# Making x + h once, along the tokens, and turning it by DMA, in a fused attention and mixer kernel

## The chip, the cores and the metric

One core of a Trainium2 chip. The engines named here are TensorE (PE, with its weight loads PEld), VectorE (DVE), ScalarE (ACT), GpSimd (POOL) and SyncE (SP), which issues the DMAs. The metric is device time in microseconds (us) of one execution; lower is better.

## The reference

Two operators in a row, for 8 batches of S = 3136 tokens, width 256, in fp32:

```
scores = (z @ z.T) / S                      # z: S x 64
x      = u * (relu(scores)**2 @ v)          # gated attention, S x 256
h      = (x.T @ U @ V).T                    # low rank 32 across the tokens
x2     = x + h
out    = x2 + relu(x2 @ w_ch1) @ w_ch2      # 256 -> 1024 -> 256
```

h needs the sum over all tokens of a batch (x.T @ U), so the second operator of a batch can start only when the batch's attention is done.

## The kernel before

**Tiling.** 3136 tokens are 24 tiles of 128 and a tail of 64. Tokens are worked on in groups of four tiles (512 tokens), so a batch has six full groups, 0 to 5, and one small group, 6, of 64 tokens. A batch and a group make an item: 56 items, and the loop over t runs nine steps longer.

**What one step t does.** The attention of item t (`av_stream`: 96 units of 256 columns, one unit being a pair of concurrent matmuls on the two halves of the array's rows; `av_end` adds the last token tile, and `av_out`, L575, multiplies by u into `x_bf`), the scores of later items (`score_burst`), the first layer `ch1_part` and the second layer `ch2_stream` (32 units) of the item eight steps back, and x + h of the item seven steps back. A small group's attention is `av_small`, its second layer `ch2_small`. Scores are squared (L301) and, where needed a second time, turned by block DMA transposes on SP (L327). In the last nine steps only the two layers run; in the first seven only attention.

**The two ways.** Each half of the rows writes one PSUM bank at a time. In way 0 half 0 writes bank 0 and half 1 bank 1, in way 1 crosswise. A stream runs all its units in one way, then the others. Between, the function `post` (L153) puts a no-op on POOL that waits for the last matmuls, and the next matmul of that accumulator waits for the no-op.

**x + h, made two ways.** `t1_all` makes t1 = x.T U once per batch. Then, for each group, h is made twice. `u2T_unit` makes it turned (features on the rows, tokens along the columns: one pair of 512 columns) and adds xT in L665; xT is `x_bf` turned by a DMA, L608, issued by `x_turn` at the start of the step before. The result `u2T` is what the first layer reads. `ch2_begin` makes h again along the tokens (two pairs of 256 columns), as the start of the second layer's accumulator. When that is full, L765 adds `x_bf` into `out_sb` (fp32) and L767 stores it.

**The order.** Nothing reorders instructions: the program emits them in the order in which a planner in Python calls them, and each engine runs its own queue in order. The planner counts PE units as time (`clock`), books estimated busy time of ACT, DVE and SP (`book`), gives out four PSUM tiles (`take_ps`) and puts off work until it is due (`hold`, `run_held`). `emit` walks the light units of a step (attention, then second layer) and puts the queues' entries (first layer, scores, x + h) at their places; an entry that needs free PSUM tiles is put off by up to 14 units until `ps_ready`. `cast` goes to ACT or DVE, whichever is booked less.

The end of a step's stream, before:

```
        qm.append((nA, -1, False, finish))             # av_end, then ch2_begin
        ...
        qm.append((nA + nC // 2, -1, False, between))  # scores, then u2T_unit
        emit((av.units if av else []) + ch2, [qc, qs, qm], av, av_box)
```

Of the kernel before, what the change touches and what calls it, by code (L numbers as in the profile page):

```python
# [18 lines left out]
def kernel(  # L19
# [52 lines left out]
    V4_bf = persist.tile([P, S], BF16, name="V4_bf")  # L72
# [3 lines left out]
    lasts, smalls, xs, t1s, u2Ts, relus = {}, {}, {}, {}, {}, {}  # L76
# [103 lines left out]
    def cast(out, in_, n):  # L180

        if free_at["act"] <= free_at["dve"]:
            book("act", clock[0], n / 110)
            nc.scalar.copy(out=out, in_=in_)  # L184
        else:
            book("dve", clock[0], n / 130)
            nc.vector.tensor_copy(out=out, in_=in_)  # L187
# [271 lines left out]
    class Ways:  # L459
        def __init__(self, total, way, step):  # L460
            self.total, self.way, self.step = total, way, step
            self.at = [0, 0]
            self.units = [self.unit] * (2 * total)
# [23 lines left out]
    def av_stream(b, g, box):  # L487
        def lhs(h, q, jt):
            jb, j = divmod(jt, GT)
            while (b, jb) not in v_cast:  # L490
                run_held(min(h[0] for h in held))
            while (b, g, jb) not in blocks:
                if (g, jb, b) in ready_turns:
                    issue_turn((g, jb, b))
                else:
                    run_held(min(h[0] for h in held))
            t = blocks[b, g, jb][1]
            if jb >= g or made_twice(b, g):
                while squared.get((b, g, jb), 0) < 2:
                    run_held(min(h[0] for h in held))  # L500
                return t[h, j, q * P : (q + 1) * P]

            return t.rearrange("p a c -> p (a c)")[h, (q * GT + j) * P : (q * GT + j + 1) * P]

        per = 2 * GT

        def step(i, way, first, least):
            if first:
                xs[b, g] = pool.tile([P, GT, D], BF16, name="x_bf", bufs=10)
                box["k"], box["ps"] = take_ps()  # L510
            jt, a = divmod(i, 2)
            pair(
                box["k"],
                crossed(
                    way,
                    a,
                    lambda h, q: dict(
                        out=four(box["ps"])[:, q, :],
                        lhsT=lhs(h, q, jt),
                        rhs=v_bfs[b][h, jt, :],  # L520
                        start=first,
                        stop=False,
                    ),
                ),
                D,
            )
            while box.get("given", 0) < least // per:
                give_block(blocks[b, g, box.get("given", 0)])
                box["given"] = box.get("given", 0) + 1

        return Ways(2 * NF, 1, step)

    def av_small(b, g):
        k, ps = take_ps()
        rows = groups[g][1]
        xs[b, g] = pool.tile([P, GT, D], BF16, name="x_bf", bufs=10)
# [65 lines left out]
    def x_turn(b, g):  # L604
        n = len(tiles_of(g))
        rows = min(P, groups[g][1])
        xT = pool.tile([P, GT, ND, P], BF16, name="xT", bufs=2)
        nc.sync.dma_start_transpose(  # L608
            out=xT[:, :n, :, :rows].rearrange("p q d c -> p (q d) c"),
            in_=xs[b, g][:rows, :n, :].rearrange("p q d -> p (q d)"),  # L610
        )
        xTs[b, g] = xT
# [25 lines left out]


    def u2T_unit(b, g):  # L640
        g0, gw = groups[g]
        n = len(tiles_of(g))
        rows = min(P, gw)
# [20 lines left out]
        u2T = pool.tile([P, ND, GT, P], BF16, name="u2T", bufs=3)  # L664
        nc.vector.tensor_tensor(  # L665
            out=u2T[:, :, :n, :rows],
            in0=ps[:, :, :gw].rearrange("p d (q c) -> p d q c", c=rows),
            in1=xTs[b, g][:, :n, :, :rows].rearrange("p q d c -> p d q c"),
            op=ALU.add,
        )  # L670
        u2Ts[b, g] = u2T

    def ch1_part(b, g, h0, way, box):

        g0, gw = groups[g]
        if way == 0:
            if h0 == 0:
                relus[b, g] = [take_block() for _ in range(NH // GT)]
            box[h0] = take_ps()
        k, ps = box[h0]  # L680
        for db in range(ND):
            ops = []
            for h in range(2):
# [7 lines left out]
                            out=ps[:, bank, :gw],  # L691
                            lhsT=w1_bf[h * hp : (h + 1) * hp, db, ht * P : (ht + 1) * P],
                            rhs=u2Ts[b, g][h * hp : (h + 1) * hp, db].rearrange("p q c -> p (q c)")[:, :gw],
# [18 lines left out]
    def ch2_begin(b, g, box):  # L712

        box["k"], box["ps"] = take_ps()
        t0 = groups[g][0] // P
        for a in range(2):
            pair(
                box["k"],
                crossed(
                    0,  # L720
                    a,
                    lambda h, q: dict(
                        out=four(box["ps"])[:, q, :],
                        lhsT=V4_bf[h, (t0 + q) * P : (t0 + q + 1) * P],
                        rhs=t1s[b][h, :],
                        start=(a == 0),
                        stop=False,
                    ),
                ),
                D,  # L730
            )

    def ch2_stream(b, g, box):
        def step(i, way, first, least):
            k, a = divmod(i, 2)
# [9 lines left out]
                        start=False,  # L745
# [7 lines left out]
            if least == 2 * NH:  # L753
                ps_free[box["k"]] = book("dve", clock[0] + 3, 11.2)
                ch2_out(b, g, four(box["ps"]), P, pool.tile([P, GT, D], FP32, name="out_sb"))

        return Ways(2 * NH, 0, step)

    def ch2_out(b, g, acc, rows, o):
# [4 lines left out]
        n, t0 = len(ts), ts[0][1]  # L764
        nc.vector.tensor_tensor(out=o, in0=acc, in1=xs[b, g][:rows, :n, :], op=ALU.add)  # L765
# [4 lines left out]
    def ch2_small(b, g):  # L770
        k, ps = take_ps()
        g0, rows = groups[g]
        nc.tensor.matmul(
            out=ps[:rows, 0, :D],
            lhsT=V4_bf[:hp, g0 : g0 + rows],
            rhs=t1s[b][:hp, :],
            start=True,
            stop=False,
            tile_position=(0, 0),
        )  # L780
        for kt in range(NH):
            c = kt % 2
            for h in range(2):
# [4 lines left out]
                    start=(kt < 2 and (h, c) != (0, 0)),  # L788
# [3 lines left out]
        pe(NH / 2 + 3)  # L792
        o = pool.tile([P, GT, D], FP32, name="out_sb")
        four_sums(k, ps, o[:rows, 1:3, :])
        ch2_out(b, g, o[:rows, 1:2, :], rows, o[:rows, 0:1, :])
        book("dve", clock[0] + 3, 3)

    def emit(light, queues, av=None, av_box=None, slack=14):
# [5 lines left out]
        def issue(queue):  # L804
            place, need, turn, unit = queue.pop(0)
            if turn and av and any(av.at):
                post(av_box["k"])
                av.turn()
            unit()
            run_held()  # L810

        queues = [sorted(q, key=lambda h: h[0]) for q in queues]
        for i, f in enumerate(light):
# [9 lines left out]
            if av and av.stuck():  # L823
# [3 lines left out]
                else:  # L827
                    post(av_box["k"])
# [49 lines left out]
    def load_V(i0):  # L878
        todo = []
        n = P // 4  # L880
        for i in range(i0, i0 + 2):
# [5 lines left out]
            def casts(i=i, entry=entry, raw=raw):  # L887
# [5 lines left out]
                if i == 3:  # L893
                    cast(V4_bf[:, NF * P :], raw[:, n * NF : n * NF + S - NF * P], 100)
# [9 lines left out]
        4: lambda: load_w(0),  # L904
        5: lambda: load_w(1) + load_U(),
# [77 lines left out]
    for t in range(n_items):  # L983
        jobs = todo[t]
        n_end = 0 if t == 0 else min(len(jobs), 2 if t % NG == NQ else 1)
        if t >= NG and t % NG == 0:
            n_end = 0
# [4 lines left out]
    for t in range(n_items + NG + 2):  # L992
# [14 lines left out]
        if 0 <= t - NG + 1 < n_items:  # L1007
            x_turn(*items[t - NG + 1])
        for i, f in enumerate(casts_next):
            hold(clock[0] + 15 + 15 * i, f)  # L1010
# [29 lines left out]
        turns_at = (16, 48, nA - 8)  # L1040
        if av and full:

            for h, x, y in zip(hs, (4, 22, 36, 62), (16, 32, 48, nA - 8)):
# [4 lines left out]
        elif av:  # L1048
# [9 lines left out]
            qs += [(x, k, True, lambda: scores(k)) for x in turns_at if k]  # L1058
        else:

            order = []
            for h in range(0, NH if mix else 0, 4):
                if att and h:
                    order.append(lambda: av_small(*att))
                order += [one(h, 0), one(h + 2, 0)] + mine[:1] + [one(h, 1), one(h + 2, 1)]
                mine = mine[1:]
            if att and not mix:
                order.append(lambda: av_small(*att))
            order += mine
            if att:  # L1070
                qc += [(0, 0, False, f) for f in order]
            else:
                n = max(nC, 1)
                qc += [(n * i / len(order) + (t == n_items) * 4, 1, False, f) for i, f in enumerate(order)]
        if u2i and u2i[1] == 0:
            qm.append((0.4 * nA, 1, False, lambda: t1_all(u2i[0])))
            if av:
                qm.append((0.7 * nA, 1, False, lambda: u2T_unit(*u2i)))

        def finish():  # L1080
            if av:
                av_end(*att, av_box)
            if nC:
                ch2_begin(*fin, ch2_box)

        def between():

            if end:
                score_burst(end)
            if u2i and att and not (av and u2i[1] == 0):  # L1090
                u2T_unit(*u2i)

        qm.append((nA, -1, False, finish))
        if u2i and not att:
            qm.append((0.4 * nC, 1, False, lambda: u2T_unit(*u2i)))
        qm.append((nA + nC // 2, -1, False, between))
        emit((av.units if av else []) + ch2, [qc, qs, qm], av, av_box)

# [29 lines left out]
```

## Time and profile before

| | |
|---|---|
| median of 3 runs | 1026.96 us (1026.88 to 1030.17) |
| profiled execution | 1027.08 us, of which its span is 1024.9 us |
| mean granted TensorE clock | 0.997 |
| PE busy | 997.8 us (97% of the span) |
| PEld, DVE, ACT busy | 778.5, 653.8 and 488.3 us |
| DMA queue q1 | 77.2% of the 16 engines' span |

Busy times are shares of the span of one execution. In a group's row, the time after the bar is the busy time and the mean of one instruction, after the second bar the idle time of its engine just before, with the work that ended it. Records of concurrent matmuls overlap, so starts tell the rate and not durations.

### The profile page before, as it was taken

The page shows a single profiled execution, that of the slowest core. Times are in us where ns is not written, and L with a number is a line of the kernel's source. Part 1 is how long each engine was busy: PE and PEld are TensorE (multiplying, and loading weights), DVE is VectorE, ACT ScalarE, POOL GpSimd, SP SyncE. Part 2 cuts the span into 40 slices and gives each one's busy share as a digit, 9 for nine tenths or more (in the row PEclk, how much of TensorE's full clock was granted, in tenths as well). Part 3 has the DMA queues.
Part 4 walks back from the last instruction along what each step waited for, and adds up shares of the span by engine and source line. Part 5 has one row for each costly group of instructions (what it writes and reads, how often), then busy time and mean ns, then how long its engine had stood idle before and what let it go on. Part 6 is the DMA issues. An engine that isn't in the chain of part 4 may idle for free.

```text
span 1024.9 us, 35526 instructions
## 1 busy us (share of the span) xinstructions
PE 997.8 (97%) x16281; PEld 778.5 (76%) x16281; DVE 653.8 (64%) x820; ACT 488.3 (48%) x547; POOL 4.0 (0%) x9
## 2 busy tenths in 40 slices
PE   5999999999999999999999999999999999999997
PEld 3878788877777777787777877777777777778665
DVE  5975865577655786557756676566765667652655
ACT  5976733456334563335533455334643456333222
POOL 1000000000000000000000000000000000000000
PEclk9999999999999999999999999999999999999999
DMA  5899999769974899759994599855997669752222
GB/s 201 164 229 257 206 214 211 161 127 212 194 172 122 178 189 199 170 98 185 201 210 130 120 205 213 170 135 139 191 230 147 143 134 180 145 114 59 76 74 87
DMA packets 341222, 168.91 MB, mean 165 GB/s; under 512 B 316496, under 2 KB 319568, under 8 KB 341072
## 3 DMA queue, kind: packets, MB, share of 16 engines
q1 hardware_dynamic: 341072, 166.64, 77.2%
q8 instruction: 127, 2.08, 0.8%
q14 instruction: 23, 0.19, 0.1%
HBM read 62.56 MB, written 25.69 MB: 86 GB/s over the span
## 4 chain that ended last, share of the span: by engine, by line
PE 90%; DVE 4%; DMA 3%; ACT 1%; issue 1%; SPq 0%; POOLq 0%; ACTq 0%; DVEq 0%
PE ps L163 88%; PE ps L542 1%; DVE blk L301 1%; DVE blk L707 1%; PE ps L620 1%; DMA blk<-blk 1%; DMA zzT<-z_bf 1%; DVE blk L307 0%; DMA xT<-x_bf 0%; DMA blk<-in_moe_V_dram 0%; DVE u_sb L563 0%; ACT u_sb L561 0%; ACT blk L311 0%; DMA out_dram<-out_sb 0%; DVE x_bf L575 0%
## 5 line engine op out<-in xcount | busy, mean ns | idle before, releaser
L163 PEld LDWEIGHTS <-blk 64*128 64x128 bf16 x12288 | 608.0, 94 | 170.0 <-POOLq L153 16.8
L163 PE MATMUL ps<-v_bf,blk 64*128 64x256 bf16 x9216 | 595.3, 269 | 5.5 <-DVE blk L301 3.3
L311 ACT ACTIVATE blk<-ps 128x1024 bf16<-128x1024 f32 x332 | 332.2, 1028 | 341.4 <-PE ps L163 329.9
L707 DVE TENSOR_SCALAR blk<-ps 128x1024 bf16<-128x1024 f32 (+1 forms) x146 | 165.6, 1134 | 206.8 <-PE ps L163 206.6
L301 DVE TENSOR_TENSOR blk<-blk 128x1024 bf16<-128x1024 bf16 x348 | 230.2, 684 | 46.0 <-ACT blk L311 45.7
L163 PE MATMUL ps<-u2T,w_bf 64*128 64x512 bf16 (+1 forms) x1792 | 235.9, 350 | 2.2 <-DVE u2T L665 2.2
L163 PE MATMUL ps<-w_bf,blk 64*128 64x256 bf16 x3072 | 193.4, 270 | 2.4 <-DVE blk L707 1.2
L163 PE MATMUL ps<-zzT 64*128 64x512 bf16 (+1 forms) x936 | 140.4, 340 | 3.3 <-DMA zzT<-z_bf 1.8
L710 ACT ACTIVATE blk<-ps 128x1024 bf16<-128x1024 f32 (+1 forms) x78 | 66.3, 851 | 115.7 <-PE ps L163 113.5
L163 PEld LDWEIGHTS <-w_bf 64*128 64x128 bf16 x1792 | 88.2, 94 | 34.6 <-issue 4.1
L665 DVE TENSOR_TENSOR u2T<-ps,xT 128x1024 bf16<-128x1024 f32 (+1 forms) x56 | 61.0, 1088 | 44.7 <-PE ps L163 42.2
L575 DVE TENSOR_TENSOR x_bf<-ps,u_sb 128x1024 bf16<-128x1024 f32 x48 | 58.7, 1224 | 19.1 <-PE ps L163 15.4
L765 DVE TENSOR_TENSOR out_sb<-ps,x_bf 128x1024 f32<-128x1024 f32 x48 | 58.7, 1224 | 4.1 <-PE ps L163 4.1
L163 PEld LDWEIGHTS <-zzT 64*128 64x128 bf16 x936 | 42.0, 94 | 10.7 <-DMA zzT<-z_bf 2.1
L311 ACT ACTIVATE last_sb<-ps 128x1024 bf16<-128x1024 f32 x23 | 23.6, 1027 | 51.4 <-PE ps L163 51.4
L307 DVE TENSOR_SCALAR blk<-ps 128x1024 bf16<-128x1024 f32 x16 | 19.6, 1223 | 7.7 <-PE ps L163 7.1
L163 PE MATMUL ps<-V_bf,t_sb 64*128 64x512 bf16 (+1 forms) x112 | 20.0, 349 | 0.0
L187 DVE CAST v_bf<-stage 128x1024 bf16<-128x1024 f32 (+1 forms) x33 | 19.8, 600 | 0.0
L163 PE MATMUL ps<-v_bf,last_sb 64*128 64x256 bf16 x192 | 18.6, 270 | 0.7
L163 PE MATMUL ps<-t_sb,V_bf 64*128 64x256 bf16 x192 | 18.8, 272 | 0.4 <-ACT blk L710 0.4
L184 ACT CAST z_bf<-stage 128x1024 bf16<-128x1024 f32 (+1 forms) x20 | 18.4, 925 | 0.4 <-DMA stage<-in_z_dram 0.4
L301 DVE TENSOR_TENSOR attn_small<-attn_small 128x1600 bf16<-128x1600 bf16 x8 | 7.9, 992 | 14.0 <-ACT attn_small L447 14.0
(52 smaller groups left out, 206.6 us busy)
## 6 DMA issues: line engine op xcount, KB each, us to landing
u_sb<-in_u_dram SPq DMA_DIRECT2D x48, 512.0 KB, 5.2
out_dram<-out_sb SPq DMA_DIRECT2D x48, 512.0 KB, 3.2
stage<-in_v_dram SPq DMA_DIRECT2D x42, 512.0 KB, 6.0
stage<-in_z_dram SPq DMA_DIRECT2D x7, 512.0 KB, 6.0
blk<-in_v_dram SPq DMA_DIRECT2D x6, 512.0 KB, 5.9
blk<-in_moe_w_ch_dram SPq DMA_DIRECT2D x4, 512.0 KB, 5.6
blk<-blk SPq DMA_TRANSPOSE x114, 5.3
stage<-in_z_dram SPq DMA_DIRECT2D x7, 256.0 KB, 6.3
```

The source lines that it names most:

```text
L163: ins = nc.tensor.matmul(**args)
L184: nc.scalar.copy(out=out, in_=in_)
L187: nc.vector.tensor_copy(out=out, in_=in_)
L301: nc.vector.tensor_tensor(out=a, in0=a, in1=a, op=ALU.mult)
L307: nc.vector.tensor_scalar(out=dst, in0=src, scalar1=scale, scalar2=0.0, op0=ALU.mult, op1=ALU.max)
L311: nc.scalar.activation(out=dst, in_=src, func=AF.Relu, scale=scale)
L542: nc.tensor.matmul(out=ps[c * hp : c * hp + rows, h, :D], lhsT=smalls[b][h * hp : (h + 1) * hp, jt, :], rhs=v_bfs[b][h * hp : (h + 1) * hp ...
L575: nc.vector.tensor_tensor(out=xs[b, g][:rows, :n, :], in0=four(box["ps"])[:rows, :n, :], in1=u_sbs[b, g][:rows, :n, :], op=ALU.mult,)
L665: nc.vector.tensor_tensor(out=u2T[:, :, :n, :rows], in0=ps[:, :, :gw].rearrange("p d (q c) -> p d q c", c=rows), in1=xTs[b, g][:, :n, :, : ...
L707: nc.vector.tensor_single_scalar(out=r, in_=ps[:, :, :gw], scalar=0.0, op=ALU.max)
L710: nc.scalar.activation(out=r, in_=ps[:, :, :gw], func=AF.Relu)
L765: nc.vector.tensor_tensor(out=o, in0=acc, in1=xs[b, g][:rows, :n, :], op=ALU.add)
```

## The change

x + h is made once per group, by the new `u2_unit`: h along the tokens (the two pairs of 256 columns that `ch2_begin` issued), and one DVE add of x into the fp32 output tile `out_sb`. The sum is then cast to bf16 over `x_bf` (`cast`) and turned by a DMA into `u2T`, now laid out tile by tile as the DMA writes it; the first layer reads it as four runs of 128 columns. Only in the last batch's group 0 is `u2T_unit` kept for the first layer, with its own xT. The second layer starts with an empty accumulator, and the output add is in place on `out_sb`.

In the order: in a step with attention and second layer, eight attention units and `av_end` come after the second layer's first half, where they were ahead of it; `av_end` now lies just before the second layer's second half. `t1_all` is at place 8 and `u2_unit` at 30 or 40; in small-group steps `u2_unit` stays between the second layer's ways. The score bursts there are left for the small group's steps alone. The first layer's last turn is four units earlier. `x_bf` has 9 buffers in place of 10, `out_sb` 3 in place of 2, and the xT pool is gone. U is loaded one step earlier, V is padded with zeros to whole tiles, and in the small group's step the casts of loaded data are due later.

```diff
+    def u2_unit(b, g, turn=True):
+        ...
+        k, ps = take_ps()
+        if n == GT:
+            for a in range(2):
+                pair(k, crossed(0, a, lambda h, q: dict(
+                            out=four(ps)[:, q, :],
+                            lhsT=V4_bf[h, (t0 + q) * P : (t0 + q + 1) * P],
+                            rhs=t1s[b][h, :],
+                            start=(a == 0), stop=(a == 1))), D)
+        ...
+        x = xs[b, g][:rows, :n, :]
+        o = pool.tile([P, GT, D], FP32, name="out_sb", bufs=3)
+        done = ps_free[k] = book("dve", clock[0] + 3, 11.2 * n / GT)
+        nc.vector.tensor_tensor(out=o[:rows, :n, :], in0=four(ps)[:rows, :n, :], in1=x, op=ALU.add)
+        u2s[b, g] = o
+        if not turn:
+            return
+        def turned():
+            u2Ts[b, g] = u2T_tile()
+            x_turn(b, g, u2Ts[b, g])
+        def down():
+            hold(cast(x, o[:rows, :n, :], n * D) + 2, turned)
+        hold(done - 3, down)
...
     def ch1_part(b, g, h0, way, box):
+        while (b, g) not in u2Ts:
+            run_held(min(h[0] for h in held))
...
-                            rhs=u2Ts[b, g][h * hp : (h + 1) * hp, db].rearrange("p q c -> p (q c)")[:, :gw],
+                            rhs=u2Ts[b, g][h * hp : (h + 1) * hp, :n, db, :rows],
...
-    def ch2_begin(b, g, box):
...
     def ch2_out(b, g, acc):
-        nc.vector.tensor_tensor(out=o, in0=acc, in1=xs[b, g][:rows, :n, :], op=ALU.add)
+        o = u2s.pop((b, g))[:rows, :n, :]
+        nc.vector.tensor_tensor(out=o, in0=acc, in1=o, op=ALU.add)
...
-        if 0 <= t - NG + 1 < n_items:
-            x_turn(*items[t - NG + 1])
+        if t == n_items - 3:
+            direct = (B - 1, 0)
+            xTs[direct] = take_block()[1][...]
+            x_turn(*direct, xTs[direct])
...
-            hold(clock[0] + 15 + 15 * i, f)
+            hold(clock[0] + (15 if g_now < NQ else 90) + 15 * i, f)
...
-            for h, x, y in zip(hs, (4, 22, 36, 62), (16, 32, 48, nA - 8)):
+            last = nA - 12
+            for h, x, y in zip(hs, (4, 22, 36, 62), (16, 32, 48, last)):
...
-            qm.append((0.4 * nA, 1, False, lambda: t1_all(u2i[0])))
+            qm.append((8 if av else 2, 1, False, lambda: t1_all(u2i[0])))
             if av:
-                qm.append((0.7 * nA, 1, False, lambda: u2T_unit(*u2i)))
+                qm.append((30, 1, False, lambda: u2_unit(*u2i)))
+            else:
+                qm.append((24, 1, False, lambda: u2T_unit(*u2i)))
+                qm.append((26, 1, False, lambda: u2_unit(u2i[0], 1)))
+        elif u2i and t == n_items + 1:
+            qm.append((0, 1, False, lambda: u2_unit(u2i[0], 0, turn=False)))
+        elif u2i and not (att and not av):
+            qm.append((40 if av else 0.4 * nC, 1, False, lambda: u2_unit(*u2i)))
         def between():
             if end:
                 score_burst(end)
-            if u2i and att and not (av and u2i[1] == 0):
-                u2T_unit(*u2i)
+            if u2i and att:
+                u2_unit(*u2i)
...
+        else:
+            qm.append((nA - 8, -1, False, lambda: None))
+            qm.append((nA + nC // 2, -1, False, lambda: av_end(*att, av_box)))
+            light = av.units[: nA - 8] + ch2[: nC // 2] + av.units[nA - 8 :] + ch2[nC // 2 :]
+        emit(light, [qc, qs, qm], av)
```

## The prediction

> **What bounds the kernel now.** I read the page's busy shares and chain first, then the table by windows for one batch, then costs from the groups (by form) and single stalls from the timeline.
>
> ```profile
> PE 997.8 (97%) x16281; PEld 778.5 (76%) x16281; DVE 653.8 (64%) x820; ACT 488.3 (48%) x547; POOL 4.0 (0%) x9
> ...
> PE 90%; DVE 4%; DMA 3%; ACT 1%; issue 1%; SPq 0%; POOLq 0%; ACTq 0%; DVEq 0%
> ```
>
> The second line is the chain that ended last: PE holds 90% of it. So the time is PE's own work plus the few places where PE stands. The windows, one batch and one full item inside it, say how few they are (columns: length, then busy time of PE, PEld, DVE, ACT, POOL, granted clock, DMA share, GB/s):
>
> ```profile
> 346.43:470.19 123.76, 123.25 (x2031) 95.46 (x2031) 81.02 (x102) 57.93 (x65) 0.00 (x0) 1.00 0.83 171
> 350.00:387.00 37.00, 36.77 (x628) 28.05 (x624) 28.72 (x41) 21.38 (x26) 0.00 (x0) 1.00 1.11 204
> 385.07:404.44 19.37, 19.37 (x314) 15.09 (x310) 11.47 (x14) 7.01 (x7) 0.00 (x0) 1.00 0.99 206
> ```
>
> PE is busy through the whole full item, DVE two thirds and ACT half of the batch; but the 16 DMA engines carry 0.83 of it, and are full in the batch's first two items (350 to 387). Work taken off PE in the body therefore shows in full, work added to DVE or ACT need not, and a new dependence on a DMA lands on the busiest helper. Start to start, two concurrent half-row matmuls (a pair) of 256 columns are 0.109 us apart here and of 512 columns 0.2175 us.
>
> **The change, part by part.** The profiled execution took 1027.08 us, a span of 1024.9 and 2.2 around it; the median is 1026.96, so the sum needs no correction between them. About 0.3% (3 us) is what a measurement of this kernel tells from no change.
>
> ```profile
> L665 DVE TENSOR_TENSOR u2T<-ps,xT 128x1024 bf16<-128x1024 f32 x48 | 58.6, 1222 | 41.2 <-PE ps L163 38.7 <-DMA xT<-x_bf 2.5
> ...
> L163 PE MATMUL ps<-V_bf,t_sb 64*128 64x512 bf16 x96 | 18.4, 376 | 0.0
> L187 DVE CAST v_bf<-stage 128x1024 bf16<-128x1024 f32 x26 | 17.8, 684 | 0.0
> L184 ACT CAST v_bf<-stage 128x1024 bf16<-128x1024 f32 x16 | 16.6, 1039 | 0.3 <-DMA stage<-in_v_dram 0.3
> ```
>
> *Removed from PE.* Before, h is made twice per full group: turned (one pair of 512, the second row) and along the tokens (two pairs of 256, on the page 192 matmuls of 272 ns). After, only the second remains, except for the last batch's group 0. 47 x 0.2175 = 10.2 us less. In the seven small-group items (av_small) the pair filled a stand that then grows by the same 0.2175: 1.5 us come back. **-8.7.**
>
> *DVE and ACT.* The add at L665 (1.22) becomes an add of the same size into fp32, which I price by the output add, L765 (1224 ns, 48 times): nothing. New are 48 casts of a full group (1.04 on ACT, 0.68 on DVE by the last two rows), some 6 per batch, beside at least 42 us idle on either engine: 0 in the body, hidden by the PE stream; if that cover is gone their time is part of the waits below. The output add in place is again 1.22. The strided first-layer operand (four runs of 128) has no row; the nearest, the first layer's and the scores' contiguous 512 columns, are 377 and 379 ns; I take 0, and the range bears some ns either way.
>
> *Way turns.* Attention and both layers run first with one pairing of array half and PSUM bank, then the other; a turn waits for a POOL semaphore. Where other work lies between, it is free. Where not, the trace shows its price:
>
> ```profile
> 363.38 1.32 PE L163 MATMUL ps<-v_bf,blk 64*128 64x256 bf16 x16
> ...
> 364.81 0.11 PEld L163 LDWEIGHTS <-last_sb 64*128 64x128 bf16 x4 [0.39 <-POOLq L153]
> 364.82 0.39 PE L163 MATMUL ps<-v_bf,last_sb 64*128 64x256 bf16 x4
> ...
> 365.05 0.49 PE L163 MATMUL ps<-v_bf,blk 64*128 64x256 bf16 x6
> ```
>
> From 363.38 to 365.05 there are ten pairs, 1.09 us of work in 1.67: 0.29 per bare turn. I counted turns with no matmul between in the emitted order of both kernels. Body: 12 before (two in each group-0 item), 38 after. Splitting the attention stream around the second layer leaves two attention pairs in the old way when the turn slips behind a PSUM buffer, in the items of groups 1, 3 and 4. 26 x 0.29 = **+7.5.** In the last items 7 before and 2 after: **-1.5.** If waits overlap more than here, 0; the range keeps that.
>
> *The first layer now waits for add, cast and DMA.* Before, the turned x came by a DMA issued an item ahead. After, the chain is matmul, add, cast, SP issue, transfer.
>
> ```profile
> DMA to landing us min/median/max: 2.4/5.5/7.6
> ```
>
> That is the turn of x from issue to landing, all 56. In a normal item some 12 us of PE work lie between the new h and the first layer: 0.2 + 1.22 + 1.04 + 5.5 = 8 fits. Not so in two places of every batch.
>
> (a) The small group's turn starts in the small item, ahead of only 2.6 us of PE work. Chain: 0.2 for the matmul, 0.42 add (the small output add), 0.3 cast, 2.4 for the shortest landing, and a little for SP: 3.5. Behind a block's transpose on SP (issue up to 5.6) it is 5 or more. I take 0.95 a time, nearest to the short landing, 7 times: **+6.6** (0 to 15).
>
> (b) Group 0's turn meets the full queue:
>
> ```profile
> 351.42 2.02 SPq L608 DMA_TRANSPOSE xT<-x_bf  x1
> ...
> 357.11 6.04 SPq L327 DMA_TRANSPOSE blk<-blk  x2
> ```
>
> The lines left out are six loads (z and v): SP issues without a gap. The new turn leaves SP behind these two block turns and lands, as the transposes there do (4.3 us), at 365 to 366, where the first layer of that group is due at 365.7. Margins for later groups are 1.3 to 2.5 us. On PE the whole stream queues behind a waiting first layer. I take 0.2 a batch, **+1.4** (0 to 14, two us a batch). [...]
>
> *Last items.* There only the two layers run, 7.6 us an item. From h to the next first layer lie some 4.0 us of PE work; the chain is 0.2 + 1.22 + 1.04 + 0.2 + 3.05 (an unloaded landing there) = 5.7. That is 1.7 us of stand, less some 0.4 of work saved or moved: +1.3 in four items, 5. The old stand goes:
>
> ```profile
> 973.77 0.79 PE L163 MATMUL ps<-u2T,w_bf 64*128 64x512 bf16 x4 [2.23 <-DVE u2T L665]
> ...
> 974.07:977.50 3.43, 3.43 (x30) 2.46 (x28) 0.00 (x0) 0.00 (x0) 0.00 (x0) 0.50 0.40 76
> ```
>
> It was 2.23 us, and 3.4 us at half clock after it (1.7 lost); but group 1's turn is now behind a small output store on SP, which I put at 3.3. With that about even, **+4** (0 to 12).
>
> *Head and the rest.* The x transposes' old wait there (some 0.5) goes; the new turns queue behind block turns at 110 to 150 us, where DMA is full: **+1** (-1 to 6). The first layer's last relu now has 1.7 us of PE work before the second layer reads it, where it had 3.5; it needs 0.2 and the 1223 ns of L707, so 0, and some 0.3 an item if ACT or DVE has a square queued ahead of it. An output tile is held from the first add to its store, a bit over an item; with three in place of two I find no add that waits for one. Moved casts and score bursts, the load of U, the padding, one x buffer less: beside PE's stream, 0.
>
> Sum: -8.7 + 7.5 - 1.5 + 6.6 + 1.4 + 4 + 1 = +10.3; 1027 + 10 = **1037 us**.
>
> **Rivals.**
>
> *Faster: the turns are hidden.* Both waits (a), (b) and the extra bare turns cost near nothing: -8.7 - 1.5 and 2 for the end, 1027 - 8 = 1019. For it: PE's stream is the bound and loses real work; the planner sees add, cast and turn and fills PE meanwhile. Against: the bare turns stand in the emitted order, with a price in the trace. If only those remain, 1026: no change. It decides whether the small group's turn lands within 2.6 us.
>
> *Much slower: the SP queue.* The turn waits in the SP queue in most full items, not in one per batch. Place: first layer's first unit, PE standing. Price: one block transpose's landing beyond its margin, 5.3 - 2 = 3 less half of what a later start relieves, 1.5 us in some 20 items, +30: 1067. For it: DMA shares of 0.99 and 1.11. Against: 12 us of cover in most items. It decides from landings of over 9 us after h.
>
> *Half clock at the end.* The granted clock fell to 0.50 after a stand of 2.23 us. If each of the four new 1.7 us stands does so, 3.4 us at half speed lose 1.7 each, +7: 1044. [...]
>
> **How the numbers follow.** Forecast with its near bounds (1030 to 1050, half clock included) 0.46; the SP queue (above 1050) 0.15; hidden 0.28; waits and savings level (1024 to 1030) 0.11. So faster 0.28, same 0.11, slower 0.61. The range of 8 in 10 reaches to the hidden case's lower side, 1015 (the -8.7 and -1.5 with nothing given back are 1017, a shorter head one or two less), and above to 1061, about half of the queue case. The slower side alone would be 1030 to 1061.
>
> **What would show it.** Right: the 512-column group on V_bf nearly gone; PE busy down some 10 us; PE idle before the u2T matmuls put down to a DMA, seven times in the small group's item and four in the last items; more PEld waits on POOLq at the stream's end. Wrong: no PE idle behind the turned u2T (hidden); or that idle in every item, some 20 times over 1 us (SP queue); or DVE adds of u2 taking other than 1.2 us.

## The result and the profile after

The changed kernel takes 1058.9 us (median of four runs, 1056.2 to 1060.9) against 1028.6 (1026.9 to 1035.2) of the kernel before: ratio 1.028, 95% interval 1.023 to 1.033. It is 30 us slower. The profiled execution took 1056.15 us with a span of 1054.4, 29.5 more than before; it is the fastest of the four, at a mean granted clock of 0.993 where the others have 0.990 or 0.991. The page of the changed kernel, busy shares and chain:

```profile
PE 997.5 (95%) x16171; PEld 767.3 (73%) x16171; DVE 647.4 (61%) x820; ACT 523.7 (50%) x604; POOL 4.0 (0%) x9
...
PE 85%; DMA 6%; DVE 4%; ACT 2%; issue 1%; SPq 0%; POOLq 0%; DVEq 0%; ACTq 0%
```

PE has 110 matmuls fewer, but its busy time hardly falls (997.8 to 997.5 us). In part that is because more of it runs at half clock: four stretches of 3.4 us at a granted clock of 0.50 while PE works, where the kernel before has one. PE's share of the chain falls from 90% to 85% while DMA's doubles. The waits of the changed kernel (engine, line, what it waited for: us in total, times, longest) name the DMA:

```profile
PEld L163 <- DMA u2T<-x_bf: 27.5, 17, 5.1
PE ps L163 <- DMA u2T<-x_bf: 22.7, 14, 4.8
PEld L163 <- POOLq L153: 21.7, 79, 0.4
```

In the kernel before, PEld's waits for POOL came to 20.5 us in 93 waits, so this sum doesn't tell a bare turn from a covered one; the start times below do.

The tile u2T's landings, and the groups that the change adds or empties (by form):

```profile
DMA to landing us min/median/max: 2.3/3.1/5.3
```

```profile
L683 DVE TENSOR_TENSOR out_sb<-ps,x_bf 128x1024 f32<-128x1024 f32 x48 | 58.7, 1223 | 69.0 <-PE ps L163 68.8
...
L183 ACT CAST x_bf<-out_sb 128x1024 bf16<-128x1024 f32 x19 | 19.7, 1039 | 2.8 <-DVE out_sb L683 2.8
L185 DVE CAST x_bf<-out_sb 128x1024 bf16<-128x1024 f32 x28 | 19.3, 690 | 0.5
...
L163 PE MATMUL ps<-V_bf,t_sb 64*128 64x512 bf16 x2 | 0.4, 382 | 0.0
```

Adds and casts cost what the rows of before said (1.22, 1.04 and 0.69 us), and the turned h is gone but for one pair. The turns land sooner than before (median 3.1 in place of 5.5). They now start at other places; issued at the places of before, in the first experiment below, the same DMAs take a median of 5.4 again.

Where the 29.5 us lie, from the starts of the eight small items' attention in both traces:

| stretch | before | after | difference |
|---|---|---|---|
| to the first small group's attention | 100.55 | 105.49 | +4.9 |
| from there to the second | 116.47 | 124.80 | +8.3 |
| the next five | 618.8 | 627.3 | +8.5 |
| the last between two | 121.68 | 121.84 | +0.2 |
| from the last small attention to the end | 67.4 | 74.9 | +7.6 |

**Body.** The timeline of a small item of the changed kernel, and of the end of a group-3 item:

```profile
361.70 0.42 DVE L683 TENSOR_TENSOR out_sb<-ps,x_bf 64x256 f32<-64x256 f32 x1 [0.65 <-PE ps L163]
362.15 0.28 DVE L185 CAST x_bf<-out_sb 64x256 bf16<-64x256 f32 x1
...
362.46 1.16 SPq L606 DMA_TRANSPOSE u2T<-x_bf  x1
...
364.81 0.23 PE L163 MATMUL ps<-u2T,w_bf 64*128 64x64 bf16 x4 [0.53 <-DMA u2T<-x_bf]
```

```profile
435.06 1.32 PE L163 MATMUL ps<-v_bf,blk 64*128 64x256 bf16 x16
436.50 0.39 PE L163 MATMUL ps<-v_bf,last_sb 64*128 64x256 bf16 x4
436.73 0.71 PE L163 MATMUL ps<-w_bf,blk 64*128 64x256 bf16 x10
```

The small group's turn goes out 0.03 us after the cast and lands 2.3 us later; PE starts its matmuls 0.80 us after the pair ahead of them where 0.1 is usual, so it loses 0.7. Ten attention pairs take 1.67 us from 435.06 to 436.73, 0.29 per bare turn, as before the change; here they stand in three items of a batch.

**Ends.** In the last items PE waits at each first layer:

```profile
1005.78 1.04 ACT L183 CAST x_bf<-out_sb 128x1024 bf16<-128x1024 f32 x1 [0.52 <-DVE out_sb L683]
...
1006.85 1.24 SPq L606 DMA_TRANSPOSE u2T<-x_bf  x1
...
1009.96 0.60 PE L163 MATMUL ps<-u2T,w_bf 64*128 64x512 bf16 x4 [1.58 <-DMA u2T<-x_bf]
```

In the head three stands come together: for the next batch's z transpose (at 80.9, 4.4 us), for a cast of v on ACT (at 120.2, 2.6) and for group 0's turn (at 129.9, 4.8). Of these, only the first was there in the kernel before, and shorter (the first line is of before, the second of after):

```profile
PE ps L163 <- DMA zzT<-z_bf: 1.8, 1, 1.8
```

```profile
PE ps L163 <- DMA zzT<-z_bf: 4.4, 1, 4.4
```

The third is a place in SP's queue: the cast of group 0's x + h ends at 116.45, and the turn leaves SP at 126.05, behind six loads and a block turn:

```profile
115.41 1.04 ACT L183 CAST x_bf<-out_sb 128x1024 bf16<-128x1024 f32 x1
...
126.05 1.77 SPq L606 DMA_TRANSPOSE u2T<-x_bf  x1
...
129.85 1.03 PE L163 MATMUL ps<-u2T,w_bf 64*128 64x512 bf16 x4 [4.80 <-DMA u2T<-x_bf]
```

Right after the first stand, and from the end of the third on, the granted clock (third column from the end) falls for 3.4 us:

```profile
80.90:84.30 3.40, 3.40 (x34) 2.46 (x36) 2.98 (x5) 0.00 (x0) 0.00 (x0) 0.56 1.44 155
128.90:132.30 3.40, 2.45 (x18) 1.31 (x20) 0.00 (x0) 0.00 (x0) 0.00 (x0) 0.53 1.08 200
```

### The profile page after: what moved, and what is told of

Read it like the earlier page. It is cut to its first block, busy times and chain, and to the rows that moved or that the text cites. A ratio compares the mean times of both kernels' runs of the same rounds, so it can differ in the third digit from the quotient of the medians.

```text
span 1054.4 us, 35367 instructions
## 1 busy us (share of the span) xinstructions
PE 997.5 (95%) x16171; PEld 767.3 (73%) x16171; DVE 647.4 (61%) x820; ACT 523.7 (50%) x604; POOL 4.0 (0%) x9
## 4 chain that ended last, share of the span: by engine, by line
PE 85%; DMA 6%; DVE 4%; ACT 2%; issue 1%; SPq 0%; POOLq 0%; DVEq 0%; ACTq 0%
PE ps L163 83%; DMA u2T<-x_bf 4%; ACT blk L310 1%; PE ps L541 1%; DVE blk L300 1%; DMA zzT<-z_bf 1%; DVE blk L765 1%; PE ps L617 1%; DMA u_sb<-in_u_dram 0%; DVE u_sb L562 0%; DVE blk L306 0%; ACT u_sb L560 0%; DVE out_sb L683 0%; PE ps L816 0%; DVE u_sb L564 0%
## 5 line engine op out<-in xcount | busy, mean ns | idle before, releaser
L163 PE MATMUL ps<-v_bf,blk 64*128 64x256 bf16 x9216 | 619.5, 270 | 8.1 <-DVE blk L300 3.3
L765 DVE TENSOR_SCALAR blk<-ps 128x1024 bf16<-128x1024 f32 (+1 forms) x114 | 132.0, 1158 | 108.7 <-PE ps L163 108.7
L768 ACT ACTIVATE blk<-ps 128x1024 bf16<-128x1024 f32 (+1 forms) x110 | 93.1, 858 | 92.4 <-PE ps L163 90.3
L683 DVE TENSOR_TENSOR out_sb<-ps,x_bf 128x1024 f32<-128x1024 f32 (+1 forms) x56 | 62.1, 1108 | 76.9 <-PE ps L163 76.8
L805 DVE TENSOR_TENSOR out_sb<-ps,out_sb 128x1024 f32<-128x1024 f32 x48 | 58.8, 1224 | 34.9 <-PE ps L163 34.9
L306 DVE TENSOR_SCALAR blk<-ps 128x1024 bf16<-128x1024 f32 x13 | 15.9, 1223 | 20.9 <-PE ps L163 20.4
L185 DVE CAST x_bf<-out_sb 128x1024 bf16<-128x1024 f32 (+1 forms) x35 | 21.3, 609 | 0.7
L183 ACT CAST x_bf<-out_sb 128x1024 bf16<-128x1024 f32 (+1 forms) x20 | 20.1, 1007 | 2.8 <-DVE out_sb L683 2.8
L183 ACT CAST v_bf<-stage 128x1024 bf16<-128x1024 f32 (+1 forms) x24 | 20.7, 869 | 0.0
L300 DVE TENSOR_TENSOR last_sb<-last_sb 128x1024 bf16<-128x1024 bf16 x24 | 16.4, 682 | 2.8 <-ACT last_sb L310 2.8
```

The source lines that it names most:

```text
L163: ins = nc.tensor.matmul(**args)
L300: nc.vector.tensor_tensor(out=a, in0=a, in1=a, op=ALU.mult)
L306: nc.vector.tensor_scalar(out=dst, in0=src, scalar1=scale, scalar2=0.0, op0=ALU.mult, op1=ALU.max)
L683: nc.vector.tensor_tensor(out=o[:rows, :n, :], in0=four(ps)[:rows, :n, :], in1=x, op=ALU.add)
L765: nc.vector.tensor_single_scalar(out=r, in_=ps[:, :, :gw], scalar=0.0, op=ALU.max)
L768: nc.scalar.activation(out=r, in_=ps[:, :, :gw], func=AF.Relu)
```

## The experiments

Each edit is made to the changed kernel (1058.9 us). The theory: PE's stream bounds the kernel, and the change puts stands into it, behind the chain add, cast, turn, and behind bare way turns. The rivals: SP and the DMA engines are too full wherever the turns stand; or the stands would only move.

**The chain cut.** The first layer reads x turned an item ahead; h is left out of the first layer's input (in the last batch's group 0 too).

```diff
+        hold(done - 3, lambda: cast(x, o[:rows, :n, :], n * D))
+        return
...
-        hold(done - 3, down)
+        return
...
+        if 0 <= t - NG + 1 < n_items:
+            e = items[t - NG + 1]
+            u2Ts[e] = u2T_tile()
+            x_turn(*e, u2Ts[e])
...
```

> The first layer reads x turned by DMA an item ahead, as the kernel before issued it, so h is left out of the first layer's input; the add, the cast and the number of turns stay. Theory (dependence): the changed kernel's 1058.9 us hold stands of PE behind add, cast and turn: 7 x 0.7 in the small items, about 4 more at group 0, 5 in the head, 1.7 in each of six last items, and a half-clock stretch after the head's; with the chain cut some 25 us go, to 1034 (1029 to 1040). Rival (load): SP and the DMA engines are just too full and any order of 56 turns costs the same: over 1052.

Measured 1036.3 (1034.6 to 1036.9); the kernel before took 1028.7 beside it. All waits of PE for u2T are gone, with as many transposes on SP. So it is the dependence and not the load: 22.6 us of the 30. In the two profiles 12.3 us of the gain lie behind the last small attention, 8.7 between the second and the last, and only 0.6 ahead of the second. In that head the stand for group 0's turn is gone, but the cast that writes over `x_bf` now waits 5.1 us on ACT for the turn that reads `x_bf`, the casts of v stand behind it, and PE waits 7.8 us for v. The later batches now take 123.87 us, against 123.76 before: the bare turns eat the PE saving.

**The bare turns.**

```diff
-            last = nA - 12
+            last = nA - 10
```

> The first layer's last unit, which turns the attention's way, is put two units later (nA - 10 in place of nA - 12). In the emitted order the body's bare turns fall from 38 to none. Theory (bare turns cost PE 0.27 us each, as the pairs of 0.38 us starts in the trace say): 38 x 0.27 = 10 us less, 1049 (1045 to 1053). Rival (PE would wait there for something else, the relu or the PSUM tile): within 3 us of 1058.9.

Measured 1046.5 (1044.6 to 1047.9), 12.4 less, for two units' difference. In the two profiles the seven stretches between small attentions are 11.9 us shorter together, 0.31 for each of the 38 turns. PEld's waits for POOL fall from 21.7 to 8.1 us, and a batch whose turns land in time but for the small group takes 122.84 us, under the 123.76 of before.

**The last items.**

```diff
-            qm.append((40 if av else 0.4 * nC, 1, False, lambda: u2_unit(*u2i)))
+            qm.append((40 if av else 0, 1, False, lambda: u2_unit(*u2i)))
```

> In the last items x + h of the next group is made at the item's start and not at 0.4 of its second layer, so some 6.5 us of PE work instead of 4 lie ahead of the first layer that reads its turn. Theory (the chain of 5.7 us has 4 of cover): four stands of 1.7 to 1.9 us go, 7 less: 1052. Rival (the last items are held by the relus or by the output tiles): less than 3 us.

Measured 1060.5 (1059.3 to 1064.7): nothing gained. The timeline says why:

```profile
1011.59 1.22 DVE L683 TENSOR_TENSOR out_sb<-ps,x_bf 128x1024 f32<-128x1024 f32 x1 [4.24 <-DMA out_dram<-out_sb]
...
1012.87 0.39 PE L163 MATMUL ps<-u2T,w_bf 64*128 64x512 bf16 x2 [3.09 <-DVE out_sb L683]
```

The earlier add finds no free output tile: it waits for a store to land, and PE behind it for the PSUM tile. So I gave it a fourth:

```diff
-        o = pool.tile([P, GT, D], FP32, name="out_sb", bufs=3)
+        o = pool.tile([P, GT, D], FP32, name="out_sb", bufs=4)
...
-        xs[b, g] = pool.tile([P, GT, D], BF16, name="x_bf", bufs=9)
+        xs[b, g] = pool.tile([P, GT, D], BF16, name="x_bf", bufs=8)
```

> As with x + h at the item's start in the last items, and with four output tiles in place of three (x buffers 8 in place of 9, to make room). With three, the add of x + h waited 4.2 us for an earlier output store to land, which took the stand's place. Theory: with the fourth tile neither wait is left in the last items; the stretch behind the last small group's attention falls from 75 to some 66 us; 1051 (1047 to 1054). Rival (a third wait, x buffers or the relus): over 1056.

Measured 1046.7 (1044.9 to 1048.5), 12.2 less; the end takes 66.1 us in place of 74.9, which is 1.3 under that of before. (Some 2 us lie in the earlier batches, where two waits for group 0's turn are shorter in this kernel's profile.)

**The first batch's plan.**

```diff
-        n_end = min(len(jobs), 2 if t > NG and t % NG == NQ else 0)
+        n_end = min(len(jobs), (2 if t % NG == NQ else 1) if 0 < t < NG else 2 if t > NG and t % NG == NQ else 0)
...
-            hold(clock[0] + (15 if g_now < NQ else 90) + 15 * i, f)
+            hold(clock[0] + (15 if g_now < NQ or t < NG else 90) + 15 * i, f)
...
```

(The lines left out put the score bursts at the stream's end back to their places of before.)

> In the first batch only, the score bursts at the stream's end, the turn's place and the casts' due times are those of the kernel before; the load of U stays early. Theory (the moved bursts push the block turns and with them the batch's z transpose back by 5 us on SP, PE stands 4.4 us for it and then runs 3.4 us at half clock): the first small group's attention starts at 101 and not at 105.5 us, and the whole is 4 to 5 us shorter, 1054. [...]

Measured 1055.6 (1053.7 to 1059.1). The first small attention starts at 101.6, 3.9 us sooner. Of that 1.8 are two half-clock stretches in the first 24 us of the changed kernel's profile, which this one does not have: the kernel with the turn's place moved, which has the changed kernel's plan and no such stretch there either, starts it at 103.7. So about 2.1 us were those of the plan (which of its parts was not tried). The wait for the z transpose falls from 4.4 to 2.3 us and that for the cast of v is gone; but PE then stands 9.6 us for group 0's turn:

```profile
114.03 0.90 SPq L204 DMA_DIRECT2D stage<-in_z_dram  x2
114.97 1.31 SPq L199 DMA_DIRECT2D stage<-in_z_dram  x2
116.33 1.23 SPq L199 DMA_DIRECT2D stage<-in_v_dram  x2
117.66 6.73 SPq L326 DMA_TRANSPOSE blk<-blk  x2
124.48 1.70 SPq L606 DMA_TRANSPOSE u2T<-x_bf  x1
```

The turn leaves SP behind six loads and two block turns. The cast ahead of it ended at 113.2, so the place in SP's queue is the wait. The second small attention starts at 229.4, where it was 230.3: what the plan gave went to the next stand.

**Cast and turn queued at once.**

```diff
-            hold(cast(x, o[:rows, :n, :], n * D) + 2, turned)
+            cast(x, o[:rows, :n, :], n * D)
+            turned()
...
-        hold(done - 3, down)
+        down()
```

> The cast and the turn are put into their queues right behind the add, not when the planner thinks their inputs are due. SP then holds the turn ahead of the block turns queued after it. Theory (in the small items PE waits for the chain itself, 0.2 + 0.4 + 0.3 + 2.3 us, and not for a place in SP's queue; at group 0 and in the head for the queue): the seven stands of 0.7 us stay, the waits of up to 2 us at group 0 and the head's 4.8 us shrink by a block turn's issue, 2 us each; 1054 (1051 to 1058). Rival (everywhere the queue): below 1050, and the small items' stands gone. Rival (ACT and SP, now waiting in order, hold up scores and loads): above 1062.

Measured 1067.3 (1066.8 to 1069.8), the third case: ACT waits 63.8 us in front of the casts for the adds, and the scores queued behind them hold PE 15 times (10.1 us). The small items' stands of 0.8 are still there, so they are the chain's length.

**The small group by PE.**

```diff
-                u2_unit(*u2i)
+                u2T_unit(*u2i)
+                u2_unit(*u2i, turn=False)
```

> For the small group alone the first layer's input is made as in the kernel before: h turned by PE (one pair of 64 columns) and x turned by DMA an item ahead; its x + h along the tokens stays, without a turn. Theory: the seven stands of 0.7 us (1.5 to 1.8 in two of them) at the first layer behind the small item go, 5 to 7 us less, 1053. Rival (they move on: the first layer then meets another wait, the relu's or the scores'): within 2 us of 1058.9.

Measured 1072.4 (1070.1 to 1073.7), 13.5 more. The stand moved: two PSUM tiles are now asked for in a row in the small item, and PE waits 1.06 us from start to start for a score's ACT pass there; and group 0's turn, ready at 250.6, now stands behind the small group's output store on SP, which waits for its own add until 253.9, so that PE stands 2.3 to 2.5 us more.

**Together.** With the turn's place, the four-tile end, the first batch's plan, and the small group's and the first group 0's input by PE:

> Together: last unit of the first layer two units later, x + h at the start of the last items with four output tiles (8 x buffers), the first batch's plan as before, the small group's first-layer input by PE, and for the first batch's group 0 likewise, with x turned an item ahead. Sum from the single ones: 1058.9 - 12.4 (measured for the place of the turn) - 8 - 4 - 5 and -7 for the head's stand and its half clock: 1022 (1017 to 1028), so below the 1028.7 of the kernel before by the PE work that the change takes off. Rival (the gains overlap, since PE then meets relus and squares): 1030 or more.

Measured 1052.4 (1046.5 to 1054.5): the small group by PE costs here too (batches of 125.8 us and more), and the first group 0's own x turn stood behind block turns on SP (PE 6.9 us behind its add). The singles don't add up.

**z loads behind the turn**, with the turn's place and the four-tile end:

```diff
+        late = b_next < B and t >= NG and g_now == 0
+        if b_next < B and not late:
             casts_next += load_part(b_next, g_now)
...
+        if late:
+            qm.append((84, 1, False, lambda: casts_next.extend(load_part(b_next, g_now))))
```

> The place of the turn two units later and the last items with four output tiles (single effects -12.4 and -12.2), and in the group-0 steps the six loads of the next batch's z and tail are put behind the turn of group 0's x + h on SP, near the step's end, in place of ahead of it. Theory (the turn of group 0 is late by its place in SP's queue): the head's stand of 4.8 us at the first layer, its half clock (1.7) and the group-0 waits of up to 2 us in some batches go; 1058.9 - 24.6 - 7 - 3 = 1024 (1020 to 1030). Rival (the two gains overlap, or the z transpose is now late instead): 1032 or more.

Measured 1046.6 (1045.4 to 1049.8): the head's stand for group 0's turn is gone (0.4), but stands of 2.3 to 3.4 us appear in five batches. The next kernel has them at the same places; there DVE's timeline names them:

```profile
255.26 0.69 DVE L185 CAST z_bf<-stage 128x1024 bf16<-128x1024 f32 x1 [4.67 <-DMA stage<-in_z_dram]
...
257.68 1.22 DVE L765 TENSOR_SCALAR blk<-ps 128x1024 bf16<-128x1024 f32 x1
```

The cast of z stands at the head of DVE's queue until its load lands, the relu (L765) behind it, and PE behind the relu for a PSUM tile.

**The small group a step sooner**, on top:

```diff
+        elif u2i and u2i[1] < NQ:
+            qm.append((40 if av else 0, 1, False, lambda: u2_unit(*u2i)))
+            if u2i[1] == NQ - 1:
+                qm.append((60 if av else 1, 1, False, lambda: u2_unit(u2i[0], NQ)))
...
-            if u2i and att:
-                u2_unit(*u2i)
```

> As the z loads behind the turn, and the small group's x + h is made one step sooner, in the step of group 5 behind that group's own, so its cast and turn have a whole small item as cover. Theory (seven stands of 0.7 us at the small group's first layer were the chain's length): 5 us less than with the z loads alone, some 1019, and below the kernel before. Rival (as with the small group by PE, another wait takes its place): no less than with the z loads alone.

Measured 1045.9 (1043.8 to 1049.5). The seven stands are gone (two waits for u2T in the whole run), and the time is the same. In the two profiles, four of the five DVE stands of this kernel are followed by half clock and one of the five in the other; three more stretches of 1.7 us lost are 5 us, as much as the seven stands were to give. (The other has one more in the last items, and its profiled execution is 2.6 us the slower.) The runs as a whole point the same way: mean granted clocks of 0.984 to 0.989 here, 0.991 to 0.994 there.

**The first batch's plan on top:**

> As the one with the small group sooner, and the first batch's plan (score bursts, place of the turn, due times of casts) as in the kernel before. Theory (that plan made the batch's first z transpose 5 us late, with a stand of 2.6 us more and a half-clock stretch): 4 us less than without, 1015. Rival (with the head's second stand gone, the first costs nothing more): within 2 us of the one without.

Measured 1045.9 (1044.9 to 1049.0), the rival's figure, but not by its reason: the wait for the z transpose falls from 4.8 to 2.5 us, and group 0's turn, now behind two block turns on SP (115.7 to 124.5 us) but no z load, is 7.3 us late again.

**The casts of z later**, on top of the small group sooner:

```diff
-            hold(clock[0] + (15 if g_now < NQ else 90) + 15 * i, f)
+            hold(clock[0] + (80 + 12 * i if g_now == 1 and t > NG else (15 if g_now < NQ else 90) + 15 * i), f)
```

> As the one with the small group sooner (1045.9 us), with the casts of z and its tail put 65 to 53 units later in the step of group 1. With the z loads behind the turn those casts stood at the head of DVE's queue until the load landed (4.7 us), with a relu behind them and PE behind the relu: a stand of 2.4 to 3.5 us in each batch but the last, and a half-clock stretch behind two of them. Theory (it is only the order on DVE): the stands and the stretches go, 6 x 2.5 + 2 x 1.7 = 18 less, 1028 (1024 to 1032), level with the kernel before, the head's z transpose (4.8) and the stands at the end being what is left over of the change's saving. Rival (the z transpose or the scores are late then): 1036 or more.

Measured 1038.6 (1037.9 to 1039.5), the best of these, 20 us under the changed kernel and still 1.0% above the kernel before (ratio 1.0096, 1.0075 to 1.0116). PE no longer waits behind the casts; it now stands 0.7 to 2.6 us for group 1's or 2's turn, which follows block turns on SP, in five batches, and half clock follows two of these stands. In its last stretch between small attentions, in which no later batch is loaded, PE waits for no turn:

```profile
850.52:970.53 120.01, 119.51 (x1998) 94.12 (x1997) 67.44 (x84) 52.61 (x62) 0.00 (x0) 1.00 0.62 124
```

That is 120.01 us against 121.68 for the same stretch before, 1.67 less: six pairs of 0.2175 (1.31) and the two bare turns of before (0.54), less 0.2 in the small item. The saving is real where every turn lands in time; that was seen only in this stretch, where the DMA engines carry 0.62 and not the 0.83 of a batch with loads.

## Why the prediction was right, and where it was not

The direction and the mechanism held: the saving on PE is there, and waits for the turn and bare turns cost more than it. The size did not: 30 us more and not 10, and the time (1058.9) lies 2 us below the range's upper end. That end was set by half of the SP-queue case and not by the head and the last items, where most of the missing 20 us lie, so it is partly luck that the range held. By its steps:

- *Removed from PE.* Right: 1.67 us less in a batch where nothing waits, 1.1 without the two bare turns; -8.7 over seven batches is 1.2 each. The sign named for it, PE busy down some 10 us, did not come: it fell by 0.3. Three more half-clock stretches, some 5 us, hide half of it; the rest is not accounted for.
- *Way turns.* Right: 0.29 each in the changed trace, and 12.4 us back when the body's 38 were removed, against 38 x 0.29 = 11.
- *(a), the small group.* Right in kind and nearly in size: 0.7 a time in four batches, 1.5 to 1.7 in three, 7.7 in all against 6.6.
- *(b), group 0's queue.* Nearly nothing in four batches, 0.3 and 2 in two. In sum the body gave +8.7 over six batches, against -8.7 + 7.5 + 6.6 + 1.4 = 6.8 for seven.
- *Last items.* Mis-sized: +7.6, with the last of the seven places of (a) in it, against 4 - 1.5 and 0.95. Six waits for the turn lie behind the last small attention, 11.0 us in all. The first (1.6) is (a)'s. Four are the normal items, as foretold; from start to start they cost 1.7 three times and 2.1 once, 7.3 together, so the 0.4 an item that I had taken off did not show. The sixth, in the transition of groups 0 and 1, is 2.8 us, beside two waits for the add of x + h (1.9 in all); I had set that transition off against the old stand as about even.
- *Head and the rest.* This is the term that failed: +1 (-1 to 6) was given, and the time to the second small attention grew by 13.3. About 1 of that is the first batch's share of the body's terms, and 1.8 are the two half-clock stretches in the first 24 us, which are not the change's. The stands and stretches that make up the rest: group 0's turn, 4.8 us; the z transpose, 4.4 us where it was 1.8; the cast of v, 2.6; two half-clock stretches, 1.7 and 1.3. The first was foreseen in its place and not in its size. The second shrinks and the third goes with the first batch's plan of before, that is with the moved bursts and casts that I had put at 0 as lying beside PE's stream. But taking one stand away there mostly moved the loss: with the chain cut the second small attention starts at 229.7, with the plan of before at 229.4, with the changed kernel at 230.3, and before at 217.0. The lowest here is 223.5, with the turn's place moved (227.0 by itself) and the z loads behind the turn.

Of the rivals, the SP queue came nearest in time but not by its place: PE waited 14 times, not in most items, and where it waited long, in the head, the queue was the cause. Half clock at the end did not come in the changed kernel's profile (granted clock 1.00 up to PE's last matmul), though six stands of 1.5 us and more lay there; in the profile of the kernel with the turn's place moved, which has the same stands there, it came twice (0.50 from 988 and from 1026 us), and the end took 78.2 us in place of 74.9. So the rival is not excluded for the runs without a profile, whose mean clocks are lower (0.990 and 0.991 against 0.993). Against "hidden" speaks the second experiment and the first: neither turns nor waits were covered.

## What to carry to other kernels

Where an engine already streams without gaps, taking 1% of its work off pays only if what replaces it depends on nothing slower: put the chain (matmul, add, cast, DMA) beside the work that lies ahead of its reader at every place, the first and last items above all, and not only in the steady one. In queues that run in order, moving a wait's cause moves the wait: each of four repairs here uncovered the next (an output tile, a store ahead on SP, a cast on DVE, the next turn). An item called free because it lies beside the bound engine needs its own place in the queues checked. And where a repair gives nothing, compare the granted clock too: one repair here, the small group sooner, took its stands away and ran at a lower mean clock (0.984 to 0.989, where it had been 0.991 to 0.994).

## What was not expected of the hardware

The granted clock did not follow a stand's length alone. Two stretches of one kernel (the small group sooner), each the 3.4 us behind a stand of PE, which was 2.7 us from start to start ahead of the first and 3.4 ahead of the second:

```profile
384.00:387.40 3.40, 3.40 (x36) 2.62 (x34) 2.10 (x3) 1.59 (x3) 0.00 (x0) 0.59 0.92 303
259.00:262.40 3.40, 3.40 (x54) 2.89 (x55) 2.96 (x4) 2.79 (x5) 0.00 (x0) 1.00 0.94 251
```

The shorter stand was followed by a granted clock of 0.59 and 36 matmuls, the longer by 1.00 and 54. The last items show the like: behind the wait of 2.8 us there the clock stayed at 1.00 in the changed kernel's profile and fell to 0.50 in that of the kernel with the turn's place moved. So a stand of 2 to 4 us was followed by a lower clock in some places of these kernels and not in others; the runs do not show what decides it.
